# Seven products in a row, then six second-product groups, with the float64 conversion cut into 56 chunks at fixed places

## The chip, the cores and the metric

The kernel runs on one core of a Trainium2 chip. The metric is the device time of one execution in microseconds (us). The engines are named as the profile names them: PE (TensorE, matmuls), DVE (VectorE), ACT (ScalarE), POOL (GpSimd) and SP, which only issues DMA transfers here. Each engine runs its own instructions strictly in program order; semaphores are the only tie between engines.

## What is computed

Local and block-summary attention over 1536 tokens gives `x`; a mixture of eight experts with Sinkhorn-balanced weights `P` follows, then a second MLP with a rational activation.

```python
# mixture of experts, x: 1536 x 512, w1: 8 x 512 x 1024, w2: 8 x 1024 x 512
for e in range(E):
    h = np.maximum(x @ w1[e], 0.0)
    out += P[:, e:e + 1] * (h @ w2[e])
# second MLP; w_in (512 x 2048) and w_out (2048 x 512) arrive as float64
h = x @ w_in
g = (a0 + a1*h + a2*h*h + a3*h**3) / (1 + |b0|*|h| + |b1|*h*h + 1e-6)
return (g @ w_out).astype(np.float32)
```

Here `np.random.randn(...) * (1.0 / np.sqrt(...))` leaves `w_in` and `w_out` in float64, so the kernel has to turn them into pairs of 32-bit numbers itself.

## The kernel before

Every factor of a matmul is held as a high and a low part (names ending in `h` and `l`), and a product is three matmuls: high by high, high by low, low by high. The stages are attention with the first expert's first half, the other expert halves (the loop this change is about), and the second MLP (units U1 and later).

**The loop.** `for v in range(NSUB): for j in range(2): block(v, j)`: 30 steps `v`, each a slice of 256 hidden columns of an expert, by two halves `j` of the tokens, 60 blocks. A block does the first matrix product of the expert by a seven-product scheme (Strassen-like): products 0 to 6, each six matmuls with 384 moving columns, into three PSUM banks X, Y, Z. ACT copies X out (`s1`, `s2`, `s3`) before the next product adds onto X; DVE adds Y or Z to these. `hidden` then takes one quarter of the result: ACT writes the high part `hh` (Relu), DVE the low part `hl`. `hidden` has an SBUF source (`s1`..`s3`) for three quarters and X for the fourth.

**Second products.** `g2w` is one group: six matmuls of 512 columns into one of three PSUM buffers (`p_v`, pool `psm`, bufs=3), then on DVE one instruction that scales by `Pt` and adds to `accs`. A block makes six such groups: three for `half` 0, three for `half` 1. They wait in the list `g2q`; `tick`, which `step` calls after a product, takes one from it. So PE's order is: product 0, one group, product 1, one group, products 2 and 3, one group, product 4, one group, product 5, one group, product 6, one group.

**Weights.** `sub_weights` is called after each product and puts the next step's weight work on POOL: in blocks with j = 0, four sums `S` (`w_sums`) and three splits (`w_op`); in blocks with j = 1, four `w_op` and two `w2_op`. A split is a POOL copy (L109) and a POOL subtraction (L110). It also issues the loads `sa` and `sb` (`dma_sub`).

**Conversion.** 64 chunks of 128 x 256 numbers. Each has five steps in the list `cvjobs`, one taken per `step` when v > 1: `cv_round` (DVE `ce`, `cm`; ACT `ch` of the chunk before), `cv_exponents` (POOL, `cf`-minus-`ch` of the chunk before, then two on `ce`), `cv_turn` (stores and the next load, SP), `cv_join` (DVE `cs`, then `cm` or `cs`), `cv_add` (DVE `cf`, two instructions). With five steps to a chunk and six ticks to a block their place in a block moves from block to block.

Two lines matter for the prediction: DVE's `cs` and `cm` of `cv_join` (L895, L898), and the accumulation L1140, which sets a `p_v` buffer free for PE.

Of the kernel before, what the change touches and what calls it, by code (L numbers as in the profile page):

```python
# [22 lines left out]
def kernel(  # L23
# [285 lines left out]
    with ExitStack() as actx:  # L309
# [18 lines left out]
        st = {}  # L328
# [272 lines left out]
        for m in (wavg[:, NB - LT // BLK:NB],):  # L601
            nc.gpsimd.memset(m, 1.0 / BLK)
            nc.gpsimd.affine_select(
                out=m, in_=m, compare_op=ALU.is_ge, fill=0.0, base=0,
# [3 lines left out]
                out=m, in_=m, compare_op=ALU.is_ge, fill=0.0, base=BLK // 2 - 1,  # L608
# [227 lines left out]
        nc.scalar.copy(dh, ps)  # L836
        nc.vector.tensor_sub(dl, ps, dh.bitcast(F32))

    CW = 256
    cvq = []  # L840
    cvs = []

    def cv_load(i):

        if i < n_in:
            r, c = divmod(i, F2 // CW)
            src, dst = w_in, [f[r * P:(r + 1) * P, c * CW:(c + 1) * CW] for f in f_in]
        else:
            r, c = divmod(i - n_in, DM // CW)
            src, dst = w_out, [f[r * P:(r + 1) * P, c * CW:(c + 1) * CW] for f in f_out]  # L850
        t = vpool.tile([P, CW, 2], U32, tag="cv", name=f"cv_{i}")
        nc.sync.dma_start(
            t, src[r * P:(r + 1) * P, 2 * c * CW:2 * (c + 1) * CW].rearrange("p (f t) -> p f t", t=2)
        )
        cvq.insert(0, (i, t, dst))

    def cv_high():
        dst, f = cvs.pop()
        h = vpool.tile([P, CW], F32R, tag="ch", name=f"ch_{len(cvjobs)}", bufs=1)
        nc.scalar.copy(h, f)  # L860
        cvs.append((dst, f, h))

    def cv_low():
        dst, f, h = cvs[-1]
        nc.gpsimd.tensor_sub(f.bitcast(F32R), f, h.bitcast(F32))  # L865

    def cv_round():

        if cvs:
            cv_high()  # L870
        i, st, dst = cvq[-1]
        lo, hi = st[:, :, 0], st[:, :, 1]
        e = vpool.tile([P, CW], U32, tag="ce", name=f"ce_{i}", bufs=1)
        m = vpool.tile([P, CW], U32, tag="cm", name=f"cm_{i}", bufs=1)
        ss = vpool.tile([P, CW], U32, tag="cs", name=f"cs_{i}", bufs=1)
        f = vpool.tile([P, CW], F32, tag="cf", name=f"cf_{i}", bufs=1)
# [23 lines left out]
    def cv_add():  # L900
        i, st, dst, e, m, ss, f = cvq[-1]
        lo = st[:, :, 0]
        nc.vector.scalar_tensor_tensor(
            out=f, in0=lo, scalar=2.0 ** -52, in1=ss.bitcast(F32), op0=ALU.mult, op1=ALU.mult
        )
        nc.vector.tensor_add(f, f, m.bitcast(F32))
        cvs.append((dst, f))
        cvq.pop()

    def cv_store():  # L910
        dst, f, h = cvs.pop()
        nc.sync.dma_start(dst[0], h.bitcast(F32))
        nc.sync.dma_start(dst[1], f)


    w_in, w_out = w_in.bitcast(U32), w_out.bitcast(U32)
    n_in = (DM // P) * (F2 // CW)
    cvjobs = []

    def cv_turn(i):  # L920
        if i:
            cv_store()
        if i + 1 < 2 * n_in:
            cv_load(i + 1)

    cvjobs += [lambda: cv_load(0)]
    for i in range(2 * n_in):
        cvjobs += [cv_round, cv_exponents, lambda i=i: cv_turn(i), cv_join, cv_add]
    cvjobs += [cv_high, cv_low, cv_store]
# [8 lines left out]
    def tick(cv=False):  # L938
# [64 lines left out]
    def w_sums(v):  # L1003
# [5 lines left out]
        nc.gpsimd.tensor_sub(S[:, 3], a12, S[:, 1])  # L1009
        wS[v] = S  # L1010

    def w_op(v, i):
        name = OPS[i]
        src = w_quarter(v, name) if name[0] == "A" else wS[v][:, int(name[1]) - 1]
        t = wpool.tile([P, 2, 2, P], F32R, tag="w1", name=f"w{name}_{v}")
        split(t[:, 0], t[:, 1], src, v == 0)
        wop[v, i] = t
# [36 lines left out]
            load_w(U1, 1, i // 2)  # L1054

    late = []

    def step(v):
        tick(v > 1)

    def block(v, j):

        n = NW
        o1, o2, ot = j * HT, j * HT + n, j * n
        X, Y, Z = (psx.tile([P, 512], F32, tag=t, name=f"{t}_{v}_{j}")[:, :n] for t in ("X", "Y", "Z"))
        s1, s2, s3 = (vpool.tile([P, n], F32, tag=t, name=f"{t}_{v}_{j}") for t in ("s1", "s2", "s3"))

        def xs(k, o):
            return lambda t: (xh[:, 2 * k + t, o:o + n], xl[:, 2 * k + t, o:o + n])

        def tt(i):
            return lambda t: (th[i][:, t, ot:ot + n], tl[i][:, t, ot:ot + n])

        def product(i, ps, get, start):
            w = wop[v, i]
            go = {} if start else {"skip_group_check": True}
            for t in range(2):
                mh, ml = get(t)
                nc.tensor.matmul(ps, lhsT=w[:, 0, t], rhs=mh, start=start and t == 0, stop=False, **go)  # L1079
                nc.tensor.matmul(ps, lhsT=w[:, 0, t], rhs=ml, start=False, stop=False, **go)  # L1080
                nc.tensor.matmul(ps, lhsT=w[:, 1, t], rhs=mh, start=False, stop=t == 1, **go)  # L1081
            sub_weights(v, j, i)

        def hidden(c, half, src):
            hh = hp["pool"].tile([P, n], F32R, tag="hh", name=f"hh_v{v}_{j}_{c}{half}")
            hl = hp["pool"].tile([P, n], F32R, tag="hl", name=f"hl_v{v}_{j}_{c}{half}")
            nc.scalar.activation(hh, src, AF.Relu)  # L1087
            nc.vector.scalar_tensor_tensor(  # L1088
                out=hl, in0=src, scalar=0.0, in1=hh.bitcast(F32), op0=ALU.max, op1=ALU.subtract
            )  # L1090
# [151 lines left out]
```

## Time and profile before

| what | value |
|---|---|
| time, median of 3 runs | 1373.31 us (1372.91 to 1373.69) |
| profiled execution, first to last instruction (span) | 1372.1 us |
| PE busy | 1358.6 us, 99% of the span |
| DVE, ACT, POOL busy | 77%, 38%, 59% |
| granted TensorE clock | 9 or more tenths in all 40 slices; mean 1.000 |
| PE's waits for others in the list of waits | 9.6 us; 5.6 of it one wait at the start |

The profile's own execution ends 1.2 us short of the median because the runs' time has something around the span. Busy shares of 99% say that PE hardly ever stands without a matmul; they don't say how far apart the matmuls start. For that the starts in the timeline are read: the distance from one start to the next.

### The profile page before, as it was taken

The page shows a single profiled execution, that of the slowest core. Times are in us where ns is not written, and L with a number is a line of the kernel's source. Part 1 is how long each engine was busy: PE and PEld are TensorE (multiplying, and loading weights), DVE is VectorE, ACT ScalarE, POOL GpSimd, SP SyncE. Part 2 cuts the span into 40 slices and gives each one's busy share as a digit, 9 for nine tenths or more (in the row PEclk, how much of TensorE's full clock was granted, in tenths as well). Part 3 has the DMA queues.
Part 4 walks back from the last instruction along what each step waited for, and adds up shares of the span by engine and source line. Part 5 has one row for each costly group of instructions (what it writes and reads, how often), then busy time and mean ns, then how long its engine had stood idle before and what let it go on. Part 6 is the DMA issues. An engine that isn't in the chain of part 4 may idle for free.

```text
span 1372.1 us, 20189 instructions
## 1 busy us (share of the span) xinstructions
PE 1358.6 (99%) x7379; PEld 1199.9 (87%) x7379; DVE 1055.3 (77%) x1828; ACT 521.1 (38%) x1164; POOL 815.7 (59%) x1051
## 2 busy tenths in 40 slices
PE   7999999999999999999999999999999999999998
PEld 6888898889998889998889898898898898888887
DVE  7985487777678767777777777777777689998885
ACT  6775412422222222222222222222222279966662
POOL 7764546777776677777777766767776012222221
PEclk9999999999999999999999999999999999999999
DMA  9530111222222222222232222222222131212102
GB/s 273 129 98 9 31 31 47 93 77 88 67 77 75 64 77 63 78 84 70 63 102 67 77 66 73 77 63 81 73 79 68 53 125 47 79 44 92 31 16 77
DMA packets 114561, 102.37 MB, mean 75 GB/s; under 512 B 24736, under 2 KB 92576, under 8 KB 114464
## 3 DMA queue, kind: packets, MB, share of 16 engines
q1 hardware_dynamic: 114464, 101.10, 24.9%
q8 instruction: 58, 0.95, 0.3%
q14 instruction: 39, 0.32, 0.1%
HBM read 81.15 MB, written 19.92 MB: 74 GB/s over the span
## 4 chain that ended last, share of the span: by engine, by line
PE 95%; DVE 2%; ACT 1%; DMA 1%; POOL 1%; issue 0%; POOLq 0%
PE p_v L186 12%; PE p_v L185 12%; PE p_v L184 12%; PE p L184 8%; PE p L186 7%; PE p L185 7%; PE X L1080 6%; PE X L1081 6%; PE X L1079 6%; PE Y L1080 3%; PE Y L1081 3%; PE Y L1079 3%; PE Z L1080 2%; PE Z L1081 2%; PE Z L1079 2%; PE sc L517 1%
## 5 line engine op out<-in xcount | busy, mean ns | idle before, releaser
L1140 DVE SCALAR_TENSOR_TENSOR accs<-p_v,Pt,accs 128x512 f32<-128x512 f32 x336 | 250.3, 745 | 82.6 <-PE p_v L186 79.2
L186 PE MATMUL p_v<-w2h_v,hl_v 128*128 128x512 f32 x720 | 285.9, 397 | 0.0
L185 PE MATMUL p_v<-w2l_v,hh_v 128*128 128x512 f32 x720 | 284.2, 395 | 0.0
L184 PE MATMUL p_v<-w2h_v,hh_v 128*128 128x512 f32 x720 | 281.6, 391 | 0.0
L1087 ACT ACTIVATE hh_v<-s 128x384 fp32r<-128x384 f32 x180 | 94.7, 526 | 316.1 <-DVE s L1102 160.2
L1088 DVE SCALAR_TENSOR_TENSOR hl_v<-s,hh_v 128x384 fp32r<-128x384 f32 x180 | 130.2, 723 | 100.8 <-ACT hh_v L1087 100.6
L234 POOL TENSOR_TENSOR hl<-ta,hh 128x512 fp32r<-128x512 f32 (+1 forms) x52 | 63.2, 1215 | 233.1 <-ACT hh L233 188.5
L186 PEld LDWEIGHTS p_v<-w2h_v,hl_v 128*128 128x128 f32 x720 | 134.9, 187 | 28.8
L184 PEld LDWEIGHTS p_v<-w2h_v,hh_v 128*128 128x128 f32 x720 | 135.3, 188 | 16.9
L185 PEld LDWEIGHTS p_v<-w2l_v,hh_v 128*128 128x128 f32 x720 | 135.0, 187 | 16.9
L109 POOL TENSOR_SCALAR wS<-S 128x256 fp32r<-128x256 f32 x116 | 51.1, 441 | 127.3 <-PE X L1081 126.1
L110 POOL TENSOR_TENSOR wS<-S,wS 128x256 fp32r<-128x256 f32 x120 | 98.8, 823 | 14.4 <-ACT wS L107 4.7
L184 PE MATMUL p<-xh,w1h 128*128 128x512 f32 (+2 forms) x288 | 103.1, 358 | 0.0
L186 PE MATMUL p<-xh,w1l 128*128 128x512 f32 (+2 forms) x288 | 101.8, 353 | 0.0
L185 PE MATMUL p<-xl,w1h 128*128 128x512 f32 (+2 forms) x288 | 101.7, 353 | 0.0
L1094 ACT COPY s<-X 128x384 f32<-128x384 f32 x60 | 28.8, 481 | 189.7 <-PE X L1081 189.7
L184 PE MATMUL p<-w2h,hh 128*128 128x512 f32 (+1 forms) x244 | 95.0, 389 | 0.5 <-DVE accs L262 0.5
L186 PE MATMUL p<-w2h,hl 128*128 128x512 f32 (+1 forms) x244 | 94.5, 387 | 0.1
L185 PE MATMUL p<-w2l,hh 128*128 128x512 f32 (+1 forms) x244 | 94.3, 386 | 0.0
L865 POOL TENSOR_TENSOR cf<-cf,ch 128x256 fp32r<-128x256 f32 x64 | 54.3, 848 | 55.8 <-ACT ch L860 55.8
L110 POOL TENSOR_TENSOR w2l_v<-sb,w2h_v 128x512 fp32r<-128x512 f32 x60 | 82.0, 1367 | 5.0
L1080 PE MATMUL Y<-xl,wS 128*128 128x384 f32 x240 | 80.9, 337 | 0.0
(213 smaller groups left out, 3397.0 us busy)
## 6 DMA issues: line engine op xcount, KB each, us to landing
sa<-in_moe_w_dram SPq DMA_DIRECT2D x30, 512.0 KB, 3.6
sb<-in_moe_w_dram SPq DMA_DIRECT2D x30, 512.0 KB, 4.0
cv<-in_moe_w_in_dram SPq DMA_DIRECT2D x32, 256.0 KB, 3.4
cv<-in_moe_w_out_dram SPq DMA_DIRECT2D x32, 256.0 KB, 3.0
f_in<-ch SPq DMA_DIRECT2D x32, 128.0 KB, 2.4
f_in<-cf SPq DMA_DIRECT2D x32, 128.0 KB, 2.4
f_out<-ch SPq DMA_DIRECT2D x32, 128.0 KB, 2.5
f_out<-cf SPq DMA_DIRECT2D x32, 128.0 KB, 2.1
```

The costliest lines, as they stand in the source:

```text
L110: nc.gpsimd.tensor_sub(lo, src, hi.bitcast(F32))
L184: nc.tensor.matmul(ps, lhsT=sh, rhs=mh, start=(i == 0), stop=False)
L185: nc.tensor.matmul(ps, lhsT=sh, rhs=ml, start=False, stop=False)
L186: nc.tensor.matmul(ps, lhsT=sl, rhs=mh, start=False, stop=(i == n_k - 1))
L234: nc.gpsimd.tensor_sub(hl[:, :n], ta, hh[:, :n].bitcast(F32))
L865: nc.gpsimd.tensor_sub(f.bitcast(F32R), f, h.bitcast(F32))
L1079: nc.tensor.matmul(ps, lhsT=w[:, 0, t], rhs=mh, start=start and t == 0, stop=False, **go)
L1080: nc.tensor.matmul(ps, lhsT=w[:, 0, t], rhs=ml, start=False, stop=False, **go)
L1081: nc.tensor.matmul(ps, lhsT=w[:, 1, t], rhs=mh, start=False, stop=t == 1, **go)
L1087: nc.scalar.activation(hh, src, AF.Relu)
L1088: nc.vector.scalar_tensor_tensor(out=hl, in0=src, scalar=0.0, in1=hh.bitcast(F32), op0=ALU.max, op1=ALU.subtract)
L1140: nc.vector.scalar_tensor_tensor(out=a, in0=ps, scalar=Pt[:, g, e:e + 1], in1=a, op0=ALU.mult, op1=ALU.add)
```

## The change

From step v = 2 on (`VG = 2`), a block issues its seven products one behind the other, in the order 0, 2, 1, 4, 3, 6, 5, and then six second-product groups: first the three of `half` 1 of the block before (`held`), then its own three of `half` 0. Product 6 goes to Z instead of onto Y, so `s2` takes one more addition. The tables `VG` and `LATER` set this; weights are made in the order of use. The conversion has 56 chunks of 296 columns, one to a block, and each step has its place: `cv_add` after product 0, `cv_high` (ACT) after product 4, `cv_low` (POOL) after product 6, stores and `cv_join` of the next chunk behind the first group, `cv_round` of the one after behind the fourth. A chunk that crosses a row of the weights is loaded and stored in two parts. The pool `h` has six buffers instead of seven.

```diff
-    hp = {"pool": wctx.enter_context(tc.tile_pool(name="h", bufs=7, side="right"))}
+    hp = {"pool": wctx.enter_context(tc.tile_pool(name="h", bufs=6, side="right"))}
...
-    CW = 256
+    CW = 296
...
+    def cv_round(i):
+        if i >= len(spans):
+            return
+        hi = cvt[i]["st"][:, :, 1]
         nc.vector.tensor_scalar(
-            out=e, in0=hi, scalar1=20, scalar2=0x7FF, op0=ALU.logical_shift_right, op1=ALU.bitwise_and
+            out=cv_tile(i, "ce"), in0=hi, scalar1=20, scalar2=0x7FF,
+            op0=ALU.logical_shift_right, op1=ALU.bitwise_and,
         )
...
+        e = cvt[i]["ce"]
         nc.gpsimd.tensor_scalar(out=e, in0=e, scalar1=896, scalar2=0, op0=ALU.subtract, op1=ALU.max)
         nc.gpsimd.tensor_scalar(out=e, in0=e, scalar1=255, scalar2=1 << 23, op0=ALU.min, op1=ALU.mult)
...
+    def cv_join(i):
+        if i >= len(spans):
+            return
+        d = cvt[i]
+        ss = cv_tile(i, "cs")
         nc.vector.scalar_tensor_tensor(
-            out=ss, in0=hi, scalar=0x80000000, in1=e, op0=ALU.bitwise_and, op1=ALU.bitwise_or
+            out=ss, in0=d["st"][:, :, 1], scalar=0x80000000, in1=d["ce"], op0=ALU.bitwise_and, op1=ALU.bitwise_or
         )
-        nc.vector.tensor_tensor(out=m, in0=m, in1=ss, op=ALU.bitwise_or)
+        nc.vector.tensor_tensor(out=d["cm"], in0=d["cm"], in1=ss, op=ALU.bitwise_or)
...
+    def cv_store(i):
+        d = cvt.pop(i)
+        for _, dst, y in cv_parts(i):
+            nc.sync.dma_start(dst[0], d["ch"].bitcast(F32)[:, y])
+            nc.sync.dma_start(dst[1], d["cf"][:, y])
...
+    VG = 2
+    LATER = [0, 2, 1, 4, 3, 6, 5]
...
+        if v >= VG:
+            k = 2 * (v - VG) + j
...
+            product(0, X, xs(0, o1), True)
+            nc.scalar.copy(s1, X)
+            cv_add(k)
+            product(2, Z, xs(1, o1), True)
+            nc.vector.tensor_add(s1, s1, Z)
+            product(1, X, tt(0), False)
+            nc.scalar.copy(s2, X)
+            hidden(0, 0, s1)
+            product(4, Y, xs(0, o2), True)
+            nc.vector.tensor_add(s2, s2, Y)
+            cv_high(k)
+            product(3, X, tt(1), False)
+            nc.scalar.copy(s3, X)
+            nc.vector.tensor_add(s3, s3, Y)
+            product(6, Z, xs(1, o2), True)
+            hidden(1, 1, s3)
+            nc.vector.tensor_add(s2, s2, Z)
+            cv_low(k)
+            product(5, X, tt(2), False)
+            hidden(0, 1, s2)
+            hidden(1, 0, X)
+            for i, f in enumerate(held + seconds_of(0)):
+                f()
+                if i == 0:
+                    cv_store(k)
+                    cv_join(k + 1)
+                elif i == max(2, len(held)):
+                    cv_round(k + 2)
+                point[0] += 1
+                run_job()
+            held[:] = seconds_of(1)
+            return
```

On PE, at the head of block v = 6, j = 0 (X and Z are the products' banks, `p_v` a second-product buffer). Before:

```order
L1081 MATMUL X_0_4080<-xh,wA_6_3801 128x384
L184 MATMUL p_v_6_4102<-w2h_v_0_3693,hh_v_1_00_3979 128x512
L185 MATMUL p_v_6_4102<-w2l_v_0_3694,hh_v_1_00_3979 128x512
L186 MATMUL p_v_6_4102<-w2h_v_0_3693,hl_v_1_00_3980 128x512
L184 MATMUL p_v_6_4102<-w2h_v_1_3720,hh_v_1_10_4042 128x512
L185 MATMUL p_v_6_4102<-w2l_v_1_3721,hh_v_1_10_4042 128x512
L186 MATMUL p_v_6_4102<-w2h_v_1_3720,hl_v_1_10_4043 128x512
L1079 MATMUL X_0_4080<-th_1791,wS_6_3833 128x384
```

And with the change:

```order
L1082 MATMUL X_0_4111<-xh,wA_6_3824 128x384
L1080 MATMUL Z_0_4113<-xh,wA_6_3845 128x384
L1081 MATMUL Z_0_4113<-xl,wA_6_3845 128x384
L1082 MATMUL Z_0_4113<-xh,wA_6_3845 128x384
L1080 MATMUL Z_0_4113<-xh,wA_6_3845 128x384
L1081 MATMUL Z_0_4113<-xl,wA_6_3845 128x384
L1082 MATMUL Z_0_4113<-xh,wA_6_3845 128x384
L1080 MATMUL X_0_4111<-th_1791,wS_6_3865 128x384
```

The 512-column group that stood between the first two products has moved behind the seventh.

On DVE, in a block (v = 3, j = 0 before; the end of v = 2, j = 1 after). Before:

```order
L1102 TENSOR_TENSOR s_3_0_3119<-s_3_0_3119,Z_0_3118 128x384
L1088 SCALAR_TENSOR_TENSOR hl_v_0_00_3181<-s_3_0_3119,hh_v_0_00_3180 128x384
L1140 SCALAR_TENSOR_TENSOR accs<-p_v_8_3194,Pt,accs 128x512
L895 SCALAR_TENSOR_TENSOR cs_3112<-cv_3037,ce_3110 128x256
L898 TENSOR_TENSOR cm_3111<-cm_3111,cs_3112 128x256
L1108 TENSOR_TENSOR s_3_0_3121<-s_3_0_3121,Y_0_3117 128x384
L1088 SCALAR_TENSOR_TENSOR hl_v_0_11_3213<-s_3_0_3121,hh_v_0_11_3212 128x384
L1140 SCALAR_TENSOR_TENSOR accs<-p_v_9_3216,Pt,accs 128x512
```

And with the change:

```order
L1089 SCALAR_TENSOR_TENSOR hl_v_1_11_3079<-s_2_1_3000,hh_v_1_11_3078 128x384
L1124 TENSOR_TENSOR s_2_1_2999<-s_2_1_2999,Z_1_2997 128x384
L1089 SCALAR_TENSOR_TENSOR hl_v_1_01_3091<-s_2_1_2999,hh_v_1_01_3090 128x384
L1089 SCALAR_TENSOR_TENSOR hl_v_1_10_3095<-X_1_2995,hh_v_1_10_3094 128x384
L1187 SCALAR_TENSOR_TENSOR accs<-p_v_3_3098,Pt,accs 128x512
L898 SCALAR_TENSOR_TENSOR cs_3109<-cv_2885,ce_2989 128x296
L901 TENSOR_TENSOR cm_2991<-cm_2991,cs_3109 128x296
L1187 SCALAR_TENSOR_TENSOR accs<-p_v_4_3112,Pt,accs 128x512
L1187 SCALAR_TENSOR_TENSOR accs<-p_v_5_3121,Pt,accs 128x512
L1187 SCALAR_TENSOR_TENSOR accs<-p_v_6_3130,Pt,accs 128x512
L881 TENSOR_SCALAR ce_3139<-cv_3014 128x296
```

The last three low parts stand together, and `cs` and `cm` always stand between the first and the second accumulation of the six.

On POOL, the end of a block with j = 1 (`w2h`, `w2l`: parts of the second weights; `S`: the sums of the next block). Before:

```order
L109 TENSOR_SCALAR w2h_v_0_3045<-sb_2758 128x512
L110 TENSOR_TENSOR w2l_v_0_3046<-sb_2758,w2h_v_0_3045 128x512
L109 TENSOR_SCALAR w2h_v_1_3071<-sb_2758 128x512
L110 TENSOR_TENSOR w2l_v_1_3072<-sb_2758,w2h_v_1_3071 128x512
L1006 TENSOR_TENSOR S_3128<-sa_3023 128x256
L1007 TENSOR_TENSOR S_3128<-S_3128,sa_3023 128x256
```

And with the change:

```order
L109 TENSOR_SCALAR w2h_v_0_3060<-sb_2762 128x512
L110 TENSOR_TENSOR w2l_v_0_3061<-sb_2762,w2h_v_0_3060 128x512
L109 TENSOR_SCALAR w2h_v_1_3072<-sb_2762 128x512
L110 TENSOR_TENSOR w2l_v_1_3073<-sb_2762,w2h_v_1_3072 128x512
L917 TENSOR_TENSOR cf_3011<-cf_3011,ch_3052 128x296
L890 TENSOR_SCALAR ce_3139<-ce_3139 128x296
L891 TENSOR_SCALAR ce_3139<-ce_3139 128x296
L999 TENSOR_TENSOR S_3175<-sa_3049 128x256
```

The conversion's three POOL instructions now always follow the second-weight splits in a block with j = 1, and the last `w_op` in one with j = 0.

## Rows read from the trace of the kernel before

**Rows 1.** Busy us (x count) of PE, PEld, DVE, ACT, POOL; granted clock; DMA
```profile
215.00:1050.00 835.00, 834.93 (x4165) 750.22 (x4164) 634.19 (x1079) 206.06 (x449) 609.41 (x773) 1.00 0.24 73
```

**Rows 2.** Timeline, PE: first matmul of two blocks, 30 blocks apart (start us, duration us)
```profile
308.58 0.33 PE L1079 MATMUL X<-xh,wA 128*128 128x384 f32 x1
...
777.78 0.33 PE L1079 MATMUL X<-xh,wA 128*128 128x384 f32 x1
```

**Rows 3.** Timeline, PE: one group of six between two products
```profile
700.62 0.39 PE L184 MATMUL p_v<-w2h_v,hh_v 128*128 128x512 f32 x1
...
702.01 0.33 PE L1079 MATMUL X<-th,wS 128*128 128x384 f32 x1
```

**Rows 4.** Timeline, PE, second MLP: runs of twelve at 512 and at 384 columns
```profile
1127.15 0.39 PE L184 MATMUL p<-w2h,hh 128*128 128x512 f32 x1
...
1129.91 0.33 PE L184 MATMUL p<-xh,w1h 128*128 128x384 f32 x1
...
1130.98 0.33 PE L184 MATMUL p<-xh,w1h 128*128 128x384 f32 x1
...
1132.02 0.39 PE L184 MATMUL p<-w2h,hh 128*128 128x512 f32 x1
...
1204.65 0.39 PE L184 MATMUL p<-w2h,hh 128*128 128x512 f32 x1
...
1207.37 0.39 PE L184 MATMUL p<-xh,w1h 128*128 128x512 f32 x1
```

**Rows 5.** Timeline, ACT, beside rows 3: a copy out of X
```profile
700.82 0.48 ACT L1094 COPY s<-X 128x384 f32<-128x384 f32 x1 [4.28 <-PE X L1081]
```

**Rows 6.** Groups by line, DVE, 215 to 1050 us (count | busy us, mean ns)
```profile
L1140 DVE SCALAR_TENSOR_TENSOR accs<-p_v,Pt,accs 128x512 f32<-128x512 f32 x314 | 233.9, 745 | 76.7 <-PE p_v L186 74.0
L1088 DVE SCALAR_TENSOR_TENSOR hl_v<-s,hh_v 128x384 fp32r<-128x384 f32 x160 | 117.1, 732 | 88.6 <-ACT hh_v L1087 88.3
...
L898 DVE TENSOR_TENSOR cm<-cm,cs 128x256 uint32<-128x256 uint32 x63 | 40.4, 642 | 2.2
L895 DVE SCALAR_TENSOR_TENSOR cs<-cv,ce 128x256 uint32<-128x256 uint32 x64 | 39.1, 611 | 0.0
```

**Rows 7.** Timeline, DVE: an addition, a low part, and the pair of cv_join twice
```profile
307.02 0.68 DVE L895 SCALAR_TENSOR_TENSOR cs<-cv,ce 128x256 uint32<-128x256 uint32 x1
307.73 1.40 DVE L898 TENSOR_TENSOR cm<-cm,cs 128x256 uint32<-128x256 uint32 x1
...
698.46 0.41 DVE L895 SCALAR_TENSOR_TENSOR cs<-cv,ce 128x256 uint32<-128x256 uint32 x1
698.90 0.42 DVE L898 TENSOR_TENSOR cm<-cm,cs 128x256 uint32<-128x256 uint32 x1
699.25 0.55 DVE L1115 TENSOR_TENSOR s<-s,Y 128x384 f32<-128x384 f32 x1
...
706.83 0.56 DVE L1088 SCALAR_TENSOR_TENSOR hl_v<-s,hh_v 128x384 fp32r<-128x384 f32 x1 [0.59 <-ACT hh_v L1087]
```

**Rows 8.** Timeline, POOL, beside the pair at 307 us
```profile
306.81 0.62 POOL L109 TENSOR_SCALAR w2h_v<-sb 128x512 fp32r<-128x512 f32 x1
307.51 1.34 POOL L110 TENSOR_TENSOR w2l_v<-sb,w2h_v 128x512 fp32r<-128x512 f32 x1
```

**Rows 9.** Groups by line, POOL, 215 to 1050 us
```profile
L110 POOL TENSOR_TENSOR wS<-S,wS 128x256 fp32r<-128x256 f32 x107 | 88.1, 823 | 8.9
...
L889 POOL TENSOR_SCALAR ce<-ce 128x256 uint32<-128x256 uint32 x64 | 70.9, 1107 | 11.1 <-DVE ce L877 11.1
...
L865 POOL TENSOR_TENSOR cf<-cf,ch 128x256 fp32r<-128x256 f32 x63 | 53.2, 845 | 55.8 <-ACT ch L860 55.8
L109 POOL TENSOR_SCALAR wS<-S 128x256 fp32r<-128x256 f32 x107 | 47.0, 439 | 109.3 <-PE X L1081 108.0
```

**Rows 10.** Timeline, PE: the first two matmuls behind a wait
```profile
851.34 0.41 PE L1079 MATMUL X<-th,wA 128*128 128x384 f32 x1
851.59 0.33 PE L1080 MATMUL X<-tl,wA 128*128 128x384 f32 x1
```

More of the change, by code (lines that the diff above doesn't have):

```diff
@@ L837, in to_x @@
         nc.vector.tensor_sub(dl, ps, dh.bitcast(F32))
-    CW = 256
-    cvq = []
-    cvs = []
-    def cv_load(i):
[L845 to L850, printed above, removed]
-        t = vpool.tile([P, CW, 2], U32, tag="cv", name=f"cv_{i}")
[L852 to L876, printed above, removed]
+    CW = 296
@@ new lines @@
+    w_in, w_out = w_in.bitcast(U32), w_out.bitcast(U32)
+    spans = []
+    for src, dst in ((w_in, f_in), (w_out, f_out)):
+        rows, cols = dst[0].shape[0] // P, dst[0].shape[1]
+        flat, o = rows * cols, 0
+        while o < flat:
+            e = min(o + CW, flat)
+            parts = []
+            while o < e:
+                r, c = divmod(o, cols)
+                w = min(e - o, cols - c)
+                parts.append((src[r * P:(r + 1) * P, 2 * c:2 * (c + w)], [f[r * P:(r + 1) * P, c:c + w] for f in dst], w))
+                o += w
+            spans.append(parts)
@@ new lines, with cv_parts, cv_tile @@
+    cvt = {}
+    def cv_parts(i):
+        o = 0
+        for src, dst, w in spans[i]:
+            yield src, dst, slice(o, o + w)
+            o += w
+    def cv_load(i):
+        if i >= len(spans):
+            return
+        t = vpool.tile([P, CW, 2], U32, tag="cv", name=f"cv_{i}")
+        n = 0
+        for src, _, y in cv_parts(i):
+            nc.sync.dma_start(t[:, y, :], src.rearrange("p (f t) -> p f t", t=2))
+            n = y.stop
+        cvt[i] = {"st": t[:, 0:n, :], "n": n}
+    def cv_tile(i, k, dt=U32, bufs=1):
+        t = vpool.tile([P, CW], dt, tag=k, name=f"{k}_{i}", bufs=bufs)[:, 0:cvt[i]["n"]]
+        cvt[i][k] = t
+        return t
@@ L903, in cv_add @@
+    def cv_add(i):
+        d = cvt[i]
+        f = cv_tile(i, "cf", F32)
         nc.vector.scalar_tensor_tensor(
-            out=f, in0=lo, scalar=2.0 ** -52, in1=ss.bitcast(F32), op0=ALU.mult, op1=ALU.mult
+            out=f, in0=d["st"][:, :, 0], scalar=2.0 ** -52, in1=d["cs"].bitcast(F32), op0=ALU.mult, op1=ALU.mult
         )
[L906 to L913, printed above, removed]
@@ L916 @@
[L916 to L929, printed above, removed]
+        nc.vector.tensor_add(f, f, d["cm"].bitcast(F32))
+        cv_load(i + 2)
@@ L930, with cv_high, cv_low @@
+    def cv_high(i):
+        nc.scalar.copy(cv_tile(i, "ch", F32R), cvt[i]["cf"])
+    def cv_low(i):
+        f = cvt[i]["cf"]
+        nc.gpsimd.tensor_sub(f.bitcast(F32R), f, cvt[i]["ch"].bitcast(F32))
+    def cv_store(i):
[3 more added lines that the diff above has]
+            nc.sync.dma_start(dst[1], d["cf"][:, y])
     jobs = []
@@ L1010, in w_sums, with turn @@
         wS[v] = S
+    VG = 2
+    LATER = [0, 2, 1, 4, 3, 6, 5]
+    def turn(v, i):
+        return LATER[i] if v >= VG else i
     def w_op(v, i):
+        i = turn(v, i)
         name = OPS[i]
@@ L1056 @@
     late = []
+    held = []
     def step(v):
-        tick(v > 1)
+        tick()
     def block(v, j):
@@ L1091, in hidden, with seconds_of @@
             ht["v", v, j, c, half] = (hh, hl)
+        def seconds_of(half):
+            return [lambda t=t: g2w(v, j, half, t) for t in range(n // P)]
+        if v >= VG:
+            k = 2 * (v - VG) + j
+            if k == 0:
+                while late:
+                    late.pop()()
+                for i in range(6):
+                    g2q.pop(0)[1]()
+                    if i in (0, 5):
+                        cv_round(i // 5)
+                    elif i == 4:
+                        cv_join(0)
+            product(0, X, xs(0, o1), True)
[29 more added lines that the diff above has]
+            held[:] = seconds_of(1)
+            return
         product(0, X, xs(0, o1), True)
@@ L1117, in block @@
         for half in range(2):
-            for t in range(n // P):
-                g2q.append((point[0] + 2, lambda half=half, t=t: g2w(v, j, half, t)))
+            g2q.extend((point[0] + 2, f) for f in seconds_of(half))
         step(v)
@@ L1191 @@
         for j in range(2):
+            if (v, j) == (VG - 1, 1):
+                cv_load(0)
+                cv_load(1)
             block(v, j)
-    assert not cvjobs
-    late.pop()()
+    assert not cvt
+    g2q += [(point[0], f) for f in held]
     while g2q or jobs:
```

21 lines of the change are left out of this document (5 added, 16 removed).

## The prediction

> **What bounds the kernel now.** I read the page's engine table first: PE is busy for 99% of the span, at full clock. Then the stretch of the loop by windows [rows 1]: in 835 us PE stands still for 0.07 us, while DVE works 634 us and POOL 609 us (73%). So the loop is bound by PE, and by nothing else; the list of waits holds no wait of PE in it that is worth a row. A change here can gain only if matmuls start closer together, and can lose as soon as PE has to wait.
>
> The timeline gives the distance between starts. Two blocks that are 30 apart start at 308.58 and 777.78 [rows 2]: 15.64 us to a block. Next, what the same matmuls take when they aren't mixed. In a run of twelve at 512 columns with equal neighbours the twelve take 2.72 us (the last two of [rows 4]), 0.2267 each. Settled 384-column matmuls take 1.04 us for six (the third and the fourth of [rows 4]), 0.1733 each. A block has 42 of these and 36 of those: 7.28 + 8.16 = 15.44 us. The missing 0.20 us is the price of changing width: a group of six that stands between products takes 1.39 us [rows 3], 0.03 over its 1.36, and there are six such groups in a block. A longer run pays little more: the twelve that follow 384-column ones take 2.76, 0.04 over (the first two of [rows 4]), and the first six products behind them 1.07, 0.03 over (the second and the third of [rows 4]).
>
> **What the grouping gives.** A block of the new kind changes width once each way: 15.44 + 0.04 + 0.03 = 15.51 us, 0.13 less. 56 blocks (v from 2 on) give **-7.5 us**. Bounds: -11.2 (no cost left at all) and 0 (the cost comes with something else than the change of width). I take -7.5 because both rows of twelve show it.
>
> The Trainium skill says otherwise ("TensorE: Matmul & The Clock Gate", section "Back-to-back issue gap"): an isolated warm matmul's gap is its columns over 2.4 plus 2.5 ns, with no term for its neighbour. By that rule grouping gives nothing and this term is 0; the rows above, with the same 512 columns at two prices, speak against it.
>
> **What the grouping takes away.** A group between two products was time in which ACT, DVE and POOL caught up. I lay one new block end to end, from its first matmul at 0. ACT starts a copy 0.20 us after the next group's first matmul and takes 0.48 [rows 3, 5]. So product 0, issued by 1.06, is out of X at 1.74, and X is wanted again at 2.10, since a product on Z lies between. The same holds for the other two copies: 0.36 us to spare each. Z is wanted again at 5.2 and `s1` has taken it by 3 or so. These waits cost nothing; without the cover each would cost the shortfall 56 times.
>
> The place where it is tight is DVE's queue behind the products. The last copy out of X (`s3`) ends at 5.90. Then, on DVE: addition 0.55 to 6.47; 0.59 until ACT has made the high part; low part 0.56 [rows 7]; addition 0.55; again 0.59 and a low part 0.56; the low part from X 0.55; the first accumulation 0.745 [rows 6]; then the pair of `cv_join`, 0.41 and 0.42 at 256 columns [rows 7], some 0.46 and 0.47 at 296; then the second accumulation. Instructions that don't need each other overlap by 0.07 (698.90 + 0.42 against 699.25 in [rows 7]). That puts the end of the second accumulation at 12.03 if nothing disturbs DVE. Who waits for it is PE: there are three `p_v` buffers, and the fifth group takes the second one's, at 7.30 + 0.04 + 4 x 1.36 = 12.78. With 0.06 for the hand-over **DVE has 0.7 us to spare**. The extra addition onto `s2` is in this chain. Before the change no row shows PE waiting for an accumulation here, because groups came one in 2.4 us or so.
>
> **What disturbs DVE is POOL.** DVE instructions with SBUF sources only are slow when POOL works beside them; the pair of `cv_join` takes 0.41 and 0.42 alone, and 0.68 and 1.40 beside the splits of the second weights [rows 7, 8], where `cm` ends 0.28 after POOL's 1.34 us instruction ends. Accumulations and additions read PSUM and keep their time. Of the chain above four instructions are open to this: two low parts and the pair. Their mean excess over the undisturbed time is 0.17, 0.17, 0.20 and 0.22 [rows 6, 7], 0.76 in sum, with POOL busy 73% of the time.
>
> Where is POOL then? In a block with j = 1 it is done with the exponents of the last `cv_round` at 1.2, and from product 0 on it has four splits (0.44 + 0.82 and 0.08 between), two second-weight splits (0.62 + 0.08 + 1.34) and `cf` minus `ch` (0.845, 0.97 at 296) [rows 8, 9]: it is busy without a gap until 11.7, so beside all four. 0.76 / 0.73 = 1.04 us of excess, 0.34 more than there is to spare. By place it is worse: the pair starts at 10.4, with the last second-weight split to 10.7 and `cf` minus `ch` to 11.7; `cs` would lose 0.2, `cm` 0.8, and the two low parts 0.47: 1.47, 0.77 too much. In a block with j = 0 POOL has sums and three splits and is done by some 9.5, before the pair; the two low parts alone cost 0.47, which fits into 0.7. So PE waits once in two blocks, in 28 blocks, before the fifth group.
>
> The size: bounds 0 (the pair falls into gaps) and 1.0 (the pair at 0.68 + 1.40, 1.25 over, and 0.47 for the low parts, less 0.7). My sketch of POOL's place is good to some 0.3 us, the mean excess is a count of 63 pairs, so I stay nearer to the mean: 0.45. A wait also costs the next start, 0.25 instead of 0.17 [rows 10]: 0.08. 28 x 0.53 = **+14.8 us** (0 to 30.8).
>
> **The rest.** Conversion work hardly changes in amount: 56 x 296 columns against 64 x 256, eight times fewer fixed parts on DVE, ACT and POOL; all of it lies off PE. `cv_store` puts its two DMAs on SP behind `sb`, which waits for POOL's last second-weight split; behind them stands only the next block's load. The stores start near 11.8 and the next `cv_add`, which writes `cf` again, is due at 16.4, so there is time for a landing; if there weren't, `cv_add` would hold DVE's queue and with it the addition that frees Z. 30 more DMAs from chunks in two parts go to the same queue, which issues some ten in 31 us. `sa` goes ahead of these stores and is wanted at the head of the next block: nothing. Six buffers in `h` suffice for two held quarters and four new ones: nothing. Once each: the six groups left over before the first new block and the three held ones after the last, which go with the transposes for the second MLP as before; between 0 and 3 us of waits for DVE, I put **+1**.
>
> Sum: -7.5 + 14.8 + 1 = +8.3 us, against the profiled execution 1372.1 + 8.3 = 1380.4; with the 1.2 us by which the median stands above the span, **1381.6 us**.
>
> **The rivals.**
>
> 1. *The port falls the other way.* If DVE's pair starts ahead of POOL's split, POOL is the one that is late, and it has slack; or POOL runs later than I sketch and the pair goes in between. Then there is no wait, and -7.5 + 1 gives 1366.8. For it: low parts at 0.56 beside a working POOL occur (the 160 average 0.73, so many are undisturbed). Against: POOL has no gap there, so DVE meets an instruction in progress nearly every time. The Trainium skill ("SBUF — State Buffer", section "SBUF: two separate sides") describes such a port of the two engines as an exclusive lock: whichever starts first keeps it for its whole instruction. By that rule this rival needs DVE first at both instructions of the pair; the 1.40 us row agrees with the lock.
> 2. *A short wait.* 0.1 to 0.3 us in 28 blocks: 1371 to 1376, about no change.
> 3. *Both kinds of block wait*, or the pair costs its full 1.25: 28 x 1.1 and more, 1393 to 1405. It decides if the j = 0 block's POOL work runs past 10.4.
> 4. *Grouping gives nothing*, the waits come all the same: 1381.6 + 7.5 = 1389.1. This is what follows if the price of rows 3 isn't that of the width.
>
> **How the numbers follow.** The forecast (1376 to 1393) has 0.50, rival 1 0.22, rival 2 0.14, rival 3 0.10, rival 4 0.04. A measurement of this kernel can tell about 0.2%, 2.7 us, from no change: slower 0.63 (forecast, 3, 4, less 0.01), same 0.14, faster 0.23. The range holds the forecast, rivals 2 and 4 and, with 1.8 us to either side for the price of the widths, most of rival 1: 1365 to 1393. For the likeliest case alone it is 1376 to 1393.
>
> **What would show it.** In the new profile: PE's distance from block to block, over two blocks, 31.02 if nothing waits, 32.1 as forecast, against 31.28 now; a run of six groups at 1.36 to 1.37 each; the wait of PE before `p_v` on DVE's accumulation, in every second block, at the fifth group; DVE's `cs` and `cm` near 1 us in those blocks and near 0.47 in the others; POOL's second-weight splits beside them. If the list of PE's waits has X, Y or Z in it, my 0.36 us for the copies was wrong; if it is empty, rival 1 holds.

## The result, and the profile after

The changed kernel takes **1383.47 us** (1382.65 to 1383.63); the ratio to the kernel before is 1.0074, 95% interval 1.0062 to 1.0086. It is 10.2 us slower by the medians. Its profiled execution spans 1381.8 us, 9.7 more than before.

The stretch of the loop by windows stands against [rows 1]. The columns are busy us (x count) of PE, PEld, DVE, ACT, POOL, then granted clock, DMA share and GB/s:

```profile
215.00:1050.00 835.00, 827.95 (x4122) 739.54 (x4121) 618.81 (x1064) 199.41 (x436) 607.15 (x742) 1.00 0.24 72
```

PE had no matmul for 7.05 us of 835, where before it was 0.07, and the stretch holds 43 matmuls fewer. DVE's and POOL's work has hardly changed. PE's list of waits, from 215 us on (line waited at, what for: us in total, times, longest), says where; the third row stands behind the loop:

```profile
PE p_v L184 <- DVE accs L1187: 5.2, 25, 0.2
PE p_v L184 <- ACT hh_v L1088: 1.3, 1, 1.3
PE x L833 <- DVE accs L1187: 0.8, 2, 0.4
PE Z L1080 <- DVE s L1112: 0.6, 1, 0.6
```

25 waits of 0.21 us make 5.2 us, about a third of the 14.6 us that the wait comes to below. That column is time in which PE shows no matmul at all; the loss is in the distance between starts. PE's timeline (start, duration), two blocks with the wait in the second:

```profile
505.63 0.33 PE L1080 MATMUL X<-xh,wA 128*128 128x384 f32 x1
...
521.14 0.33 PE L1080 MATMUL X<-xh,wA 128*128 128x384 f32 x1
...
533.70 0.39 PE L186 MATMUL p_v<-w2h_v,hl_v 128*128 128x512 f32 x1
534.30 0.50 PE L184 MATMUL p_v<-w2h_v,hh_v 128*128 128x512 f32 x1 [0.21 <-DVE accs L1187]
534.64 0.40 PE L185 MATMUL p_v<-w2l_v,hh_v 128*128 128x512 f32 x1
...
537.15 0.33 PE L1080 MATMUL X<-xh,wA 128*128 128x384 f32 x1
```

The block with j = 0 takes 15.51 to 15.53 us, the one with j = 1 takes 16.01: 31.53 for the two, against 31.28 before [rows 2]. In the second the fifth group starts 0.60 after the matmul ahead of it, where 0.23 is usual, and the next start is 0.34 later instead of 0.23: 0.37 + 0.11 us lost, in a place where the list shows 0.21. This is the wait that the prediction named, at the group it named, in the blocks it named.

DVE's timeline shows what the wait was for, in the block with j = 1 (first six rows) and in the next one, with j = 0:

```profile
529.84 0.56 DVE L1089 SCALAR_TENSOR_TENSOR hl_v<-s,hh_v 128x384 fp32r<-128x384 f32 x1 [0.59 <-ACT hh_v L1088]
530.32 0.55 DVE L1089 SCALAR_TENSOR_TENSOR hl_v<-X,hh_v 128x384 fp32r<-128x384 f32 x1
530.78 0.74 DVE L1187 SCALAR_TENSOR_TENSOR accs<-p_v,Pt,accs 128x512 f32<-128x512 f32 x1
531.44 1.14 DVE L898 SCALAR_TENSOR_TENSOR cs<-cv,ce 128x296 uint32<-128x296 uint32 x1
532.61 0.98 DVE L901 TENSOR_TENSOR cm<-cm,cs 128x296 uint32<-128x296 uint32 x1
533.51 2.06 DVE L1187 SCALAR_TENSOR_TENSOR accs<-p_v,Pt,accs 128x512 f32<-128x512 f32 x3
...
545.86 1.23 DVE L1089 SCALAR_TENSOR_TENSOR hl_v<-s,hh_v 128x384 fp32r<-128x384 f32 x1 [0.59 <-ACT hh_v L1088]
...
548.13 0.45 DVE L898 SCALAR_TENSOR_TENSOR cs<-cv,ce 128x296 uint32<-128x296 uint32 x1
548.61 0.47 DVE L901 TENSOR_TENSOR cm<-cm,cs 128x296 uint32<-128x296 uint32 x1
549.00 2.06 DVE L1187 SCALAR_TENSOR_TENSOR accs<-p_v,Pt,accs 128x512 f32<-128x512 f32 x3
```

Three accumulations stand in one row of 2.06 us; the first of the three, which sets free the buffer of the fifth group, ends at 533.51 + 0.745 = 534.25, and PE starts at 534.30. The pair takes 2.15 us there and 0.95 in the block with j = 0. POOL beside it, in the block with j = 1:

```profile
529.90 0.98 POOL L109 TENSOR_SCALAR w2h_v<-sb 128x512 fp32r<-128x512 f32 x1
530.96 1.29 POOL L110 TENSOR_TENSOR w2l_v<-sb,w2h_v 128x512 fp32r<-128x512 f32 x1
532.21 1.05 POOL L917 TENSOR_TENSOR cf<-cf,ch 128x296 fp32r<-128x296 f32 x1
```

POOL's second row ends at 532.25, and `cs` at 532.58; the third ends at 533.26, and `cm` at 533.59. Each of the pair ends 0.33 us after the POOL instruction that was running when it started, as the `cm` of [rows 7, 8] did by 0.28. The same holds, at 0.32 to 0.33 us, for `cs` and `cm` in all 24 blocks with j = 1 between 300 and 1050 us. The section on the chip calls semaphores the only tie between engines; these rows show another, since what POOL runs beside a DVE instruction can set when it ends. The first row shows the other way round: the low part at 529.84 started ahead of POOL's copy and kept its 0.56, and the copy took 0.98 instead of the 0.62 of [rows 8].

The rest of the loss is in the first new blocks. PE's timeline in the first of them:

```profile
230.70 0.40 PE L186 MATMUL p_v<-w2h_v,hl_v 128*128 128x512 f32 x1
232.36 0.47 PE L184 MATMUL p_v<-w2h_v,hh_v 128*128 128x512 f32 x1 [1.26 <-ACT hh_v L1088]
```

In all the first groups of that block lose 1.85 us between starts, and a wait at Z in the third new block 1.07 (from 257.14 on).

### The profile page after: what moved, and what is told of

It reads as the page before. It is cut to its first block, busy times and chain, and to the rows that moved or that the text cites. A ratio compares the mean times of both kernels' runs of the same rounds, so it can differ in the third digit from the quotient of the medians.

```text
span 1381.8 us, 20312 instructions
## 1 busy us (share of the span) xinstructions
PE 1360.8 (98%) x7379; PEld 1197.0 (87%) x7379; DVE 1050.4 (76%) x1836; ACT 516.8 (37%) x1156; POOL 819.6 (59%) x1027
## 4 chain that ended last, share of the span: by engine, by line
PE 78%; DVE 13%; ACT 4%; DMA 2%; POOL 1%; issue 1%; SPq 0%; DVEq 0%; POOLq 0%; ACTq 0%
PE p_v L184 9%; PE p_v L186 8%; PE p_v L185 8%; PE p L184 7%; PE p L186 7%; PE p L185 7%; PE X L1082 5%; PE X L1080 5%; PE X L1081 5%; DVE hl_v L1089 3%; DVE accs L1187 3%; PE Z L1080 2%; PE Z L1081 2%; PE Z L1082 2%; ACT hh_v L1088 2%; DVE cs L898 2%
## 5 line engine op out<-in xcount | busy, mean ns | idle before, releaser
L184 PE MATMUL p_v<-w2h_v,hh_v 128*128 128x512 f32 x720 | 285.2, 396 | 6.6 <-DVE accs L1187 5.2
L186 PE MATMUL p_v<-w2h_v,hl_v 128*128 128x512 f32 x720 | 281.8, 391 | 0.1
L1187 DVE SCALAR_TENSOR_TENSOR accs<-p_v,Pt,accs 128x512 f32<-128x512 f32 x336 | 241.5, 744 | 36.8 <-PE p_v L186 35.6
L1089 DVE SCALAR_TENSOR_TENSOR hl_v<-s,hh_v 128x384 fp32r<-128x384 f32 x180 | 119.0, 661 | 147.6 <-ACT hh_v L1088 147.6
L890 POOL TENSOR_SCALAR ce<-ce 128x296 uint32<-128x296 uint32 (+1 forms) x56 | 67.5, 1205 | 203.8 <-DVE ce L881 203.8
L110 POOL TENSOR_TENSOR wS<-S,wS 128x256 fp32r<-128x256 f32 x120 | 104.1, 868 | 14.4 <-ACT wS L107 4.7
L1082 PE MATMUL X<-th,wS 128*128 128x384 f32 x240 | 80.2, 334 | 0.0
L1081 PE MATMUL X<-tl,wS 128*128 128x384 f32 x240 | 80.2, 334 | 0.0
```

The lines of the kernel that those rows point to most:

```text
L110: nc.gpsimd.tensor_sub(lo, src, hi.bitcast(F32))
L184: nc.tensor.matmul(ps, lhsT=sh, rhs=mh, start=(i == 0), stop=False)
L186: nc.tensor.matmul(ps, lhsT=sl, rhs=mh, start=False, stop=(i == n_k - 1))
L1089: nc.vector.scalar_tensor_tensor(out=hl, in0=src, scalar=0.0, in1=hh.bitcast(F32), op0=ALU.max, op1=ALU.subtract)
L1187: nc.vector.scalar_tensor_tensor(out=a, in0=ps, scalar=Pt[:, g, e:e + 1], in1=a, op0=ALU.mult, op1=ALU.add)
```

## The experiments

The first six runs each change one thing in the changed kernel. The theory is the prediction's: the loss is a wait for a `p_v` buffer, which comes free late because POOL stretches `cs` and `cm`. Block times are distances between the first matmuls of blocks in PE's timeline; in nearly all blocks from 300 to 1050 us they repeat to 0.05 us, without waits to 0.001. Ratios are to the kernel before, run again beside these runs (medians 1373.59 and 1373.74 us). Six of the runs are single; the repeats of the changed kernel and of the first, second and eighth run lie within 1.3 us of each other.

**1. The pair behind the third group.**

```diff
                 if i == 0:
                     cv_store(k)
+                if i == 2:
                     cv_join(k + 1)
-                elif i == max(2, len(held)):
+                if i == max(2, len(held)):
                     cv_round(k + 2)
```

> The changed kernel with cv_join of the next chunk issued behind the third of the six groups, not the first; all else as it is. Theory (the pair cs, cm, made slow by POOL, stands ahead of the accumulation that the fifth group waits for): the 0.37 + 0.11 us at the fifth group goes in all blocks with j = 1, both kinds of block take 15.52 to 15.55 us, and the time is 1383.5 - 28 x 0.48 = 1370 us (1369 to 1371.5). The low parts and the accumulations keep their times; cs and cm run about 2.1 us later. Rival (the queue of DVE is too long as a whole, so that work that is moved back only moves the wait to the sixth group or to the next block's first accumulation): blocks with j = 1 stay near 16.0 and the time is above 1378.

Measured: 1369.86 us (1369.56 to 1370.79), ratio to the kernel before 0.9976 (0.9966 to 0.9985). Both kinds of block take 15.507 us, and no wait for `accs` is left in the steady loop. DVE's timeline in a block with j = 1:

```profile
528.83 0.46 DVE L898 SCALAR_TENSOR_TENSOR cs<-cv,ce 128x296 uint32<-128x296 uint32 x1
529.33 0.47 DVE L901 TENSOR_TENSOR cm<-cm,cs 128x296 uint32<-128x296 uint32 x1
```

Started 2 us later, behind POOL's last instruction, the pair also costs less than half. Moving one call by two groups turns the loss into a gain. The run doesn't tell the length of DVE's chain from POOL's part in it, since it takes the pair out of the chain altogether.

**2. Five buffers.** The fourth and fifth group of a block go to the two banks of pool `psb`, which are idle in the loop.

```diff
...
-                f()
+                f((psb, "g") if 3 <= i < 5 else (psm, "mm"))
...
```

> The changed kernel with the fourth and the fifth of a block's six groups written into the two PSUM banks of pool psb, which nothing else uses in this stretch, so that a second-product group has five buffers instead of three; DVE's and POOL's order and work are as they were, and cs and cm stay slow. Theory (PE waits for a buffer, and for nothing else that DVE makes late): no wait at the fifth group, 15.52 to 15.55 us for every block, 1370 us (1369 to 1371.5). Rival (the lateness of DVE is carried on): the wait turns up again at the sixth group or at the next block's X or Z, in blocks with j = 1 that stay above 15.8, and the time is above 1378.

Measured: 1369.77 us (1369.03 to 1370.23), ratio 0.9971 (0.9962 to 0.9981); 15.507 us for every block. DVE's timeline, j = 1:

```profile
526.33 1.14 DVE L898 SCALAR_TENSOR_TENSOR cs<-cv,ce 128x296 uint32<-128x296 uint32 x1
527.50 0.97 DVE L901 TENSOR_TENSOR cm<-cm,cs 128x296 uint32<-128x296 uint32 x1
```

The pair is as slow as before, and it costs nothing. So PE's loss is the wait for a buffer and no general lateness of DVE: with the buffer there, DVE catches up within the block.

**3. No cf-minus-ch on POOL.** `cv_low` is empty; the low parts of the converted weights are left out.

> The changed kernel without the POOL subtraction cf minus ch of the conversion (cv_low empty), so the low parts of the converted weights are not made; every instruction of DVE and PE is there. Theory (POOL's instruction beside it is what stretches cm): cm in blocks with j = 1 goes from 0.98 to about 0.47 while cs, which stands beside the second-weight split, stays near 1.1; the chain ends 0.5 earlier, the wait of 0.37 is gone or below 0.05, and the time is 1370 to 1372. Rival (the chain itself is too long, with its extra addition onto s2): the wait stays near 0.37 and the time near 1383.

Measured: 1370.99 us in one run; blocks 15.527 and 15.507, no wait for `accs` in PE's list. DVE's and POOL's timelines, j = 1:

```profile
527.48 1.13 DVE L898 SCALAR_TENSOR_TENSOR cs<-cv,ce 128x296 uint32<-128x296 uint32 x1
528.65 0.47 DVE L901 TENSOR_TENSOR cm<-cm,cs 128x296 uint32<-128x296 uint32 x1
...
527.00 1.29 POOL L110 TENSOR_TENSOR w2l_v<-sb,w2h_v 128x512 fp32r<-128x512 f32 x1
```

DVE's instructions and their order are unchanged. `cm`, which now has no POOL instruction beside it, falls from 0.98 to 0.47; `cs`, which still has one, stays at 1.13. The rival, that the chain is too long by itself (its extra addition onto `s2`), falls: the chain is whole, and of the 0.5 us that blocks with j = 1 had lost 0.02 is left.

**4. POOL kept busy where it was idle.** In blocks with j = 0 the last subtraction of the weights is repeated four times behind `cv_low`.

```diff
+            if j == 0 and v + 1 < NSUB:
+                y = wop[v + 1, 1]
+                for q in range(4):
+                    nc.gpsimd.tensor_sub(y[:, 1], wS[v + 1][:, 1], y[:, 0].bitcast(F32))
```

> The changed kernel with four more POOL subtractions of 256 columns (about 0.74 us each) behind cv_low in the blocks with j = 0, repeating the last one of the weight's split, so that POOL is busy there to some 12.4 us after the block's start, beside cs and cm; results and all other engines' work are the same. Theory: cs and cm in these blocks go from 0.45 and 0.47 to 0.7 to 1.2 each, the chain that had 0.24 us to spare is late by 0.3 to 1.1, blocks with j = 0 get a wait at the fifth group too and take 15.9 to 16.8 us; the time is 1393 to 1418. Rival (POOL beside them isn't the cause): cs and cm keep 0.45 and 0.47, no wait there, and the time stays at 1383.

Measured: 1401.38 us in one run; blocks with j = 0 now take 16.18 us nearly throughout, the others 16.02, hardly more than the 16.01 before the edit. DVE and POOL in a block with j = 0, and PE in the one two blocks earlier:

```profile
555.16 0.70 DVE L898 SCALAR_TENSOR_TENSOR cs<-cv,ce 128x296 uint32<-128x296 uint32 x1
555.89 0.90 DVE L901 TENSOR_TENSOR cm<-cm,cs 128x296 uint32<-128x296 uint32 x1
...
553.65 3.73 POOL L1129 TENSOR_TENSOR wS<-S,wS 128x256 fp32r<-128x256 f32 x4
...
525.30 0.50 PE L184 MATMUL p_v<-w2h_v,hh_v 128*128 128x512 f32 x1 [0.38 <-DVE accs L1191]
```

The pair grows by 0.68 us with nothing changed on DVE, and PE waits at the fifth group there too. With the third run this is POOL's effect both taken away and added. The Trainium skill ("SBUF — State Buffer", section "SBUF: two separate sides") describes the port that DVE and GpSimd share as an exclusive lock, held for a whole instruction by whoever starts first; the pair's ends 0.33 us behind POOL's agree with that.

**5 and 6. More runs of 512 columns in a block.** These ask what a change of width costs. In the fifth run the three held groups stand one by one between products, in the sixth in one run of three behind the third product; in both only the block's own three are left behind the seventh.

> The changed kernel with the three held groups one by one behind the second, the fourth and the sixth product and only the block's own three in a run behind the seventh; the same matmuls, four runs of 512 columns in a block instead of one. The wait at the fifth group should be gone, as the accumulations are spread. Theory (each change of width costs, 0.033 us for a single group, 0.033 to 0.066 for the run): 15.44 + 3 x 0.033 + 0.03 to 0.07 = 15.57 to 15.61 us per block, against 15.507 with one run and no wait; the time is 1373 to 1376. Rival (the gap has no term for the neighbour and the gain of the new blocks came from elsewhere): 15.51 per block, 1370.

> The changed kernel with the three held groups in a run behind the third product and the block's own three in a run behind the seventh: two runs of 512 columns in a block. It asks what a run pays, whatever its length. If a run of any length pays 0.066, as one of 36 does: 15.44 + 0.13 = 15.57 us per block. If a run of three pays 0.033, as a single group does: 15.51, the same as one run. By the rule without a neighbour's term: 15.51 too, so the runs of e5 decide between those. No wait is expected at the groups; X, Y and Z aren't late, since a run of three gives the other engines 4 us.

Measured: 1428.35 and 1506.32 us, one run each. Both expectations missed the time by far, because I had overlooked what the held groups do: they are the cover for the low and high parts of the block's own quarters. PE's timeline of the fifth run, first a single held group between products, then the block's own groups:

```profile
540.92 0.39 PE L184 MATMUL p_v<-w2h_v,hh_v 128*128 128x512 f32 x1
...
542.31 0.33 PE L1080 MATMUL X<-th,wS 128*128 128x384 f32 x1
...
548.18 0.50 PE L184 MATMUL p_v<-w2h_v,hh_v 128*128 128x512 f32 x1 [0.49 <-ACT hh_v L1088]
548.52 0.40 PE L185 MATMUL p_v<-w2l_v,hh_v 128*128 128x512 f32 x1
549.50 0.50 PE L186 MATMUL p_v<-w2h_v,hl_v 128*128 128x512 f32 x1 [0.58 <-DVE hl_v L1089]
```

The single group takes 1.39 us as before [rows 3], so the price is there. But the blocks take 15.96 us (j = 0) and 17.24 (j = 1), not 15.6: behind the seventh product PE waits for ACT's high part and DVE's low part in the first group. The sixth run has the same waits, longer, and a further loss on top, told of at the end.

**7. The same question with cover.** From the kernel with five banks, one held group is moved behind the third product, two stay.

```diff
+            if held:
+                held.pop(0)()
             product(4, Y, xs(0, o2), True)
```

> The kernel with five banks, and one of the three held groups moved from behind the seventh product to behind the third; two held groups stay as cover for the block's own three, so that no wait is expected. Theory (a single group between products pays 0.029 and the products behind it 0.004): 15.507 + 0.033 = 15.540 us per block, and 56 x 0.033 = 1.8 us more than with five banks: 1371.6. Rival (no term for the neighbour): 15.507 and 1369.8. If two held groups don't cover (low part from X is ready some 2.4 us after the seventh product, wanted after 3.9), waits of PE for hh or hl appear at the third group and this run tells nothing of the price.

Measured: 15.540 us for every block, against 15.507 with five banks, and no wait in the loop behind the first new block: 0.033 a block, as the theory had it. PE's timeline at the moved group:

```profile
503.37 0.39 PE L184 MATMUL p_v<-w2h_v,hh_v 128*128 128x512 f32 x1
...
504.75 0.33 PE L1080 MATMUL Y<-xh,wS 128*128 128x384 f32 x1
```

These two starts lie 1.39 us apart before rounding; six such matmuls cost 1.36 when they stand in the long run. The whole time, 1369.64 in one run, isn't above the 1369.77 with five banks, though the expectation had 1371.6: this kernel has no wait at Z in its third new block, which with five banks cost 1.49 (that block took 16.99), so the two nearly cancel (56 x 0.033 = 1.85). The profiled executions differ by what is left, 1367.9 against 1367.5 us.

**8 and 9. A version that beats both kernels.** Five banks, the pair behind the third group, the load `sb` issued behind the block's stores, and of the six groups left over before the first new block only three run ahead of it, the other three are held (the first `cv_round` and `cv_join` calls move with them):

```diff
+                cv_round(0)
                 while late:
                     late.pop()()
-                for i in range(6):
+                for i in range(3):
                     g2q.pop(0)[1]()
...
+                held[:] = [f for _, f in g2q]
+                g2q.clear()
```

> The changed kernel with five buffers for the groups (as in the run with five banks), cv_join behind the third group, three of the six groups left over before the first new block held instead of run ahead of it, and the load sb issued behind the two stores of the block, not ahead of them. Theory: 15.507 us per block without waits, as with five banks (1369.8), and the once-only waits of the first blocks go: 1.4 to 1.9 us at the first block's groups, where no held group covers the low parts, and 1.5 at Z in the third new block, where cv_add waits for the store of the chunk before: 1366.4 to 1367.5 us, ratio to the kernel before 0.995. Rival (these waits only move, as DVE has the same work in these blocks): 1368.5 to 1370.

Measured: **1366.83 us** (1366.55 to 1367.59), ratio to the kernel before 0.9951 (0.9937 to 0.9964). All of PE's waits from 215 to 1120 us:

```profile
PE x L833 <- DVE accs L1191: 0.8, 2, 0.4
PE p L186 <- POOL hl L234: 0.2, 1, 0.2
```

Every new block takes 15.507 us, up to the last step `v`, where the transposes for the second MLP begin. The ninth run asks whether the place of `sb` had a part in it:

> The version with all four edits, but the load sb issued where the changed kernel has it, ahead of the block's two stores. If sb ahead of the stores is what made cv_add wait for the store in the third new block: a wait at Z of 0.6 to 1.8 us there comes back, and the time is 1367.6 to 1368.7. If the wait at the first new block's groups had pushed the stores late instead: no wait at Z, 1366.8.

Measured: 1366.63 us in one run, the same block times, no wait at Z. So `sb` ahead of the stores doesn't make the wait at Z by itself. Of the edits that are left, five banks and the later pair each left a wait at Z in its own run (1.0 and 1.3 us); what was added is the three held groups. Without them the first new block has three groups instead of six and takes 13.29 us in place of 15.5, so POOL's subtraction, the stores behind it and the next `cv_add` all fall later in their blocks. The store of `cf` in the second new block, and the `cv_add` that waits for it, with five banks (first two rows, block from 235.39 us) and in the ninth run (block from 234.22):

```profile
250.52 0.42 SPq L923 DMA_DIRECT2D f_in<-cf  x1
254.92 0.83 DVE L906 SCALAR_TENSOR_TENSOR cf<-cv,cs 128x296 f32<-128x296 uint32 x1 [2.87 <-DMA f_in<-cf]
...
246.42 0.42 SPq L923 DMA_DIRECT2D f_in<-cf  x1
250.93 0.47 DVE L906 SCALAR_TENSOR_TENSOR cf<-cv,cs 128x296 f32<-128x296 uint32 x1 [0.18 <-DMA f_in<-cf]
```

`cv_add` starts 4.4 to 4.5 us behind the issue both times; the issue comes 15.1 us into its block without the held groups and 12.2 with them. That the held groups alone bring this about was not tried.

## Why the prediction was right

**The sum.** Forecast -7.5 + 14.8 + 1 = +8.3 for the profiled execution; it came out at +9.7.

| term | forecast | measured |
|---|---|---|
| grouping, 56 blocks | -7.5 (15.51 a block) | -7.4 (15.507, second run) |
| wait in blocks with j = 1 | +14.8 (0.53 x 28) | +14.6 (31.533 less 31.013 is 0.52 for two blocks) |
| once only | +1 (0 to 3) | +2.5 (the rest: 1.85 and 1.07 at two places, less some 0.4 for two blocks with a shorter wait) |

By the medians it is +10.2: the median stands 1.7 us above the span here (1383.47 and 1381.8), not 1.2 as I had put. One sign was summed wrongly: two blocks at 32.1 us don't follow from the forecast, since 31.02 + 0.53 = 31.55, and 31.53 came out.

**The price of the width** was right, in its size and in its parts: a run of 36 pays 0.041 at its head and the 42 products behind it 0.026, a single group 0.029 and the six products behind it 0.004. In the sixth run one of 18 pays 0.041, and the products behind it 0.026. So two runs cost twice as much as one; what counts is how many changes there are and, by 0.034 us, whether a stretch is a single group of six. The rule that the Trainium skill ("TensorE: Matmul & The Clock Gate", section "Back-to-back issue gap") gives for an isolated matmul has no term for the neighbour and would have had this term at zero; the seventh run and the 15.507 us blocks speak against it for this stream.

**The wait** was right in place, cause and sum, and its size was 0.37 + 0.11 against 0.45 + 0.08. Inside the term the parts were off, and that they made up for each other is luck:

- The chain, undisturbed: forecast to end at 12.03 after the block's first matmul (the terms named there add up to 11.97). In the block with j = 0 the second accumulation ends 12.59 after it (549.00 + 0.745, less 537.15), 0.67 of that from one stretched low part: 11.92. PE wanted the buffer at 12.79 (534.30 less 0.37 and 521.14), forecast 12.78. To spare, less 0.05 for the hand-over: 0.82, forecast 0.7.
- By place I had the two low parts at +0.47, `cs` at +0.2 and `cm` at +0.8: 1.47. They were 0, +0.68 and +0.51: 1.19. The low part at 529.84 came ahead of POOL's instruction and kept 0.56; `cs` met the second-weight split with 0.81 us to go (531.44 to 532.25), not 0.3, because POOL itself ran 0.4 us later than in my sketch (done at 533.26, 12.1 after the block's start; sketched 11.7). 1.19 less 0.82 is 0.37, the 0.37 that PE lost.
- The measured 1.19 lies between the mean excess by POOL's busy share (1.04) and the count by place (1.47). The count by place needs POOL's position to better than the 0.3 us that I gave it; the mean does not.

**Once only** was mis-sized. I had said that the leftover groups go as before; the first new block has no held groups in front of its own three, so PE waits for its high and low parts, 1.85 us, and the wait at Z comes two blocks later. The cover of the held groups was in no sentence of the prediction, because in the steady block it is never short.

**The rest** held: no wait for X or Y, ACT's copies in time; POOL with j = 0 done at 9.5 (546.67 less 537.15), as sketched. The stores were in time but for once, when `cv_add` stood 2.74 us behind a landing in the third new block.

**The rivals.** The port the other way (1): it happened to a low part, but `cs` and `cm` lost to POOL throughout the steady loop. The short wait (2) and both kinds of block (3): no; rival 3 is what the fourth run made of the blocks with j = 0, at 1401 us (its lower end, 1393, is below its own sum, 1366.8 + 30.8 = 1397.6). Grouping that gives nothing (4): no.

## What to carry to other kernels

When work is regrouped to make one engine's stream denser, lay the other engines' chain end to end against the buffer that the dense stream will want next, and count what a neighbour on a shared port can add; here 0.82 us to spare met 1.19. Look then for the one instruction in that chain that nobody waits for, and move it behind the one that is waited for, or give the stream another buffer: they were worth 13.6 and 13.7 us here. And ask of anything "held over" what it covers, above all in the first round, where there is nothing held yet.

## What was not expected of the hardware

In the sixth run PE's clock fell in the middle of a block. Windows of that trace (us; PE, PEld, DVE, ACT, POOL busy; granted clock; DMA, GB/s):

```profile
536.00:539.00 3.00, 1.67 (x8) 0.87 (x6) 2.41 (x3) 0.90 (x2) 2.92 (x4) 1.00 0.44 153
539.00:540.00 1.00, 0.41 (x2) 0.30 (x2) 0.65 (x2) 0.00 (x0) 0.85 (x1) 1.00 0.31 31
540.00:541.00 1.00, 1.00 (x5) 0.78 (x4) 0.76 (x2) 0.00 (x0) 0.00 (x0) 0.83 0.40 82
541.00:542.00 1.00, 1.00 (x3) 0.78 (x3) 0.83 (x2) 0.00 (x0) 0.00 (x0) 0.50 0.87 268
...
544.00:545.00 1.00, 1.00 (x6) 0.92 (x6) 0.43 (x1) 0.00 (x0) 0.00 (x0) 0.97 0.00 0
```

PE's timeline at the place:

```profile
538.38 0.51 PE L184 MATMUL p_v<-w2h_v,hh_v 128*128 128x512 f32 x1 [1.33 <-ACT hh_v L1088]
...
539.70 0.50 PE L186 MATMUL p_v<-w2h_v,hl_v 128*128 128x512 f32 x1 [0.59 <-DVE hl_v L1089]
...
540.79 0.63 PE L184 MATMUL p_v<-w2h_v,hh_v 128*128 128x512 f32 x1
541.21 0.63 PE L185 MATMUL p_v<-w2l_v,hh_v 128*128 128x512 f32 x1
```

PE had stood still for 1.33 and 0.59 us before it, and from 540.7 to 544.1 the granted clock is 0.50, the 1.2 GHz level: starts of 512 columns are 0.427 apart instead of 0.227, 1.6 us lost beside the waits themselves. Of the 27 blocks with j = 1 that have these two waits 16 show it and take 19.64 us; the other eleven, with the same waits, take 18.04. So the two waits alone don't settle whether the clock falls, and what does is not shown. In the fifth run, with waits of 0.49 and 0.58 at the same matmuls, and in the changed kernel, with one short wait, the clock stays at 1.00.
